# Output stores through GpSimd's queue and diagonal sums on VectorE, with a new hand-written order

## The chip, the core and the metric

The kernel runs on one core of one Trainium2 chip. The metric is the device time of one execution in microseconds (us), and for each kernel the median of its runs. The core's engines are TensorE (PE, with its weight loads as PEld), VectorE (DVE), ScalarE (ACT), GpSimd (POOL) and SyncE (SP, which here only issues DMAs). Each works through its own list of instructions in order and waits on semaphores for the others.

## What is computed

Two parts, one after the other. The first is a linear attention with a decaying state, for 4 batches, 8 heads, 768 steps and 48 dimensions. The second is a feed-forward layer of 384 to 2048 to 384 with a squared ReLU, on the attention's output of 3072 tokens.

```python
for t in range(S):                       # attention, all batches b and heads h
    cur = einsum('bhd,bhe->bhde', u[None] * kt, vt)
    y[:, :, t] = einsum('bhd,bhde->bhe', rt, state + cur)
    state = w[None, :, :, None] * state + einsum('bhd,bhe->bhde', kt, vt)
...
h = x @ w_in                             # x: 3072 x 384, from y
r = maximum(h, 0.0)
out = (r * r) @ w_out                    # 3072 x 384, float32
```

The product with u concerns a step's own k and v alone: for each token and head it is the sum over d of r·u·k, times v. This is the "diagonal" below.

## The kernel before

The 768 steps are cut into 6 chunks of 128, so that there are 24 units of one chunk and one batch: unit i has chunk i // 4 and batch i % 4. For each unit:

- r and k are loaded (`rt`, `kt`) and scaled by powers of w into one bf16 tile `rkw` (`scale`, L301 for two units at a time from unit 6 on, L303 for units 0 to 5, by VectorE).
- `rkw` is transposed into `rkT`: units 0 to 5 by TensorE (`turn`, L333, with an eviction by ScalarE, L337), later pairs by one transposing DMA (`rkD`, L322).
- `at` (L369) multiplies k and r into scores, `mask` (L377, VectorE, two per unit) keeps those before the diagonal.
- The diagonal: VectorE multiplies the two halves of `rkT` into `rk` (L357 for a pair, L360 for one unit), and four small TensorE matmuls with `uwb`, a table of u/w, add up over d: in `diag_sums` (L389) for units 0 to 3, and inside `sums` (L410), ahead of the state's product (L398), for units 4 to 23. `diag_v` (`dv`, L420) multiplies the sums with v.
- `y_mm` (`y`, L441 and L447) multiplies the scores with v and r with the state; `evict_y` (`yb`, L456) adds the diagonal's part. `yb` is transposed into `xT`: by TensorE for units 0 to 5 (`xturn`), later by a transposing DMA (`xD`, L467).
- `state_add`, `state_decay` and `state_cast` (`sadd`, `sdec`, `stb`) carry the state on.
- `mm1` (L493) is x times `w_in`, 16 blocks per unit or pair, in pieces; `relu` (L501, ScalarE), then the square by ScalarE (`sqA`, L508) or VectorE (`sqD`, L510); `mm2` (L517; L533 for the last unit, in two column ranges) is the product with `w_out`. `evict_o` (`osb`, L524) copies the result to one of six buffers named osb, and `store` (`out`, L553) writes it to the output from SP's queue.

What runs when is written out by hand. A manual schedule records the instructions in the order of the string `ORDER`; each engine gets its own part of that order. A word such as `m1.6.3@5` is the step, the unit, the piece and the PSUM bank. `fill.8` is eight matmuls of a constant tile (L216) that do nothing but keep TensorE occupied.

The loads of r and k come from SP's queue. POOL's queue carries the weights (`w_in_q`, L288, and `w_out_q`, L291, which are converted to bf16 on the way), `vt` of units 0 to 5 (L311) and two small loads (L168 and L169). A DMA that waits on SP or POOL holds up all that are behind it on the same engine.

Of the kernel before, what the change touches and what calls it, by code (L numbers as in the profile page):

```python
# [16 lines left out]
kt.0.0 kt.0.1 rt.0.0 rt.1.0 I.0 rt.1.1 vt.0 ktA.1.0 lnat.0 fill.26 log@4567 kt.1.1 lnat.1 ids rt.2.0 w.1 upper w.0  # L17
fill.8 cols@1 rt.2.1 wk scale.0.0 kt.2.0 zeros scale.0.1 wr fill.8 turn.0.0@2 kt.2.1 copied uwb turn.0.1@5 rkT.0.0
rt.3.0 rkT.0.1 vt.1 rk.0 fill.10 at.0@63 scale.1.0 rt.3.1 I.3 kb.0@4 mask.0.0 d.0@2 turn.1.0@7 I.2 kbT.0 kt.3.0
mask.0.1 rkT.1.0 vt.2 scale.1.1 vb.0 I.1 kt.3.1 fill.19 turn.1.1@4 dv.0 y.0@3 rkT.1.1 rt.4.0 yb.0 vb.1 rk.1 fill.9  # L20
kb.1@4 kt.4.0 scale.2.0 at.1@31 xturn.0@6 rt.4.1 mask.1.1 d.1@5 turn.2.0@2 xT.0 rkT.2.0 scale.2.1 kt.4.1 fill.5
m1.0.0@7 kbT.1 mask.1.0 turn.2.1@2 relu.0.0 dv.1 rt.5.0 fill.2 y.1@1 rkT.2.1 m1.0.3@4 yb.1 end rt.5.1 s.1@5
scale.3.0 relu.0.3 wend xturn.1@7 rk.2 at.2@26 xT.1 kb.2@0 mask.2.1 sqA.0.0 kt.5.0 d.2@4 turn.3.0@3 vt.3 s.0@7
sadd.1 rkT.3.0 m1.0.2@1 kt.5.1 scale.3.1 kbT.2 O.0 m1.1.0@6 mask.2.0 vb.2 relu.0.2 vt.4 turn.3.1@3 dv.2 m1.1.3@5
rt.6 rkT.3.1 sadd.0 O.1 y.2@1 relu.1.0 kt.6 m1.1.2@0 yb.2 relu.1.3 vt.5 at.3@72 rk.3 relu.1.2 kb.3@4 mask.3.1
xturn.2@6 sqA.1.0 O.2 m1.0.1@5 scale.4.0 xT.2 s.2@0 O.3 sqD.0.3 d.3@2 relu.0.1 m1.1.1@1 vb.3 mask.3.0 turn.4.0@3
kbT.3 m1.2.0@6 scale.4.1 relu.1.1 dv.3 m1.2.1@4 rkT.4.0 sqD.1.3 sqA.0.2 y.3@7 m1.2.2@1 scale.5.0 relu.2.1 sqD.1.1
m1.2.3@2 relu.2.2 sqD.0.1 s.3@5 sqA.1.2 turn.4.1@4 m2.0.0@3 sadd.3 relu.2.3 sadd.2 m2.1.0@1 rkT.4.1 yb.3 relu.2.0
m2.1.1 rk.4 vb.4 scale.5.1 kb.4@7 stb.1 xturn.3@6 at.4@42 kbT.4 m2.0.1 mask.4.1 xT.3 stb.0 s.4@5 mask.4.0 turn.5.0@6
m1.3.0@2 sqD.2.1 rkT.5.0 y.4@0 dv.4 relu.3.0 turn.5.1@6 rt.8 sadd.4 m1.3.3@7 rkT.5.1 yb.4 m2.1.2 sqA.3.0 sqA.2.0  # L30
m2.0.2 kt.8 xturn.4@2 m2.0.3 xT.4 scale.6.0 kb.5@5 osb.0 m2.1.3 scale.7.0 relu.3.3 m1.3.1@2 vtS.6 kbT.5 vb.5
m1.4.0@6 scale.6.1 scale.7.1 at.5@75 relu.4.0 m2.2.0@0 mask.5.0 osb.1 rkD.6 sqA.4.0 m1.4.1@4 sqD.2.3 sqA.2.2 sqD.3.3
m1.4.2@1 relu.3.1 mask.5.1 m2.2.1 stb.3 sdec.4 m1.4.3@6 relu.4.2 rt.10 rk.5 y.5@5 sqA.4.2 scale.8.0 s.5@2 scale.8.1
relu.4.1 m2.2.2 scale.9.0 relu.4.3 vtS.8 m1.3.2@1 sqD.3.1 stb.4 m2.3.0@4 dv.5 relu.3.2 yb.5 m2.2.3 scale.9.1 kt.10
m2.3.1 osb.2 sadd.5 sqA.4.1 m2.4.0@1 sqD.4.3 vb.6 xturn.5@0 sdec.5 at.6@2376 xT.5 rk.6 rkD.8 m2.4.1 stb.2 mask.7.0
stb.5 m1.5.0@0 sqA.3.2 mask.6.0 s.7@7 relu.5.0 mask.7.1 m1.5.3@5 mask.6.1 s.6@2 relu.5.3 m2.4.2 dv.6 out.0 vb.8
y.6@3 dv.7 rt.12 y.7@0 yb.6 m1.5.1@6 yb.7 m2.3.2 sadd.6 relu.5.1 xD.6 scale.10.0 m2.4.3 sqA.5.0 scale.10.1 sqA.5.1
m2.3.3 sadd.7 vtS.10 osb.4 m1.5.2@6 scale.11.1 scale.11.0 m2.5.0@3 relu.5.2 sqD.5.3 kt.12 m2.5.1 sqA.5.2 rk.8
at.8@1520 osb.3 sdec.6 m2.5.2 mask.9.0 rkD.10 m2.5.3 mask.8.0 s.8@4 mask.8.1 osb.5 s.9@2 m1.6.0@7 mask.9.1 m1.6.1@6
sadd.8 relu.6.0 dv.9 kt.14 m1.6.3@5 relu.6.1 dv.8 m1.6.7@1 sqA.6.0 scale.12.0 sadd.9 sqA.6.1 y.9@3 rt.14 y.8@4 vb.10  # L40
m1.6.2@0 yb.8 stb.6 m1.6.5@2 yb.9 relu.6.3 sdec.9 xD.8 m1.6.4@6 relu.6.5 scale.12.1 m2.7.0@3 relu.6.2 sqD.6.3
relu.6.7 vtS.12 m2.6.0@4 scale.13.0 relu.6.4 scale.13.1 m1.6.6@7 sqA.6.2 rk.10 at.10@6120 sqA.6.4 rkD.12 m2.6.1
relu.6.6 mask.10.0 sqA.6.5 s.10@5 sdec.7 m2.7.1 sqA.6.6 sqD.6.7 m2.7.2 stb.7 mask.10.1 stb.9 out.1 m2.7.3 sadd.10
kt.16 mask.11.0 y.10@6 osb.7 m1.8.0@1 dv.10 m1.8.1@2 rt.16 scale.14.0 relu.8.0 sdec.8 m1.8.3@5 relu.8.1 mask.11.1
m2.6.2 stb.8 yb.10 sqA.8.1 s.11@3 y.11@2 relu.8.3 dv.11 m1.8.6@1 vb.12 yb.11 m1.8.4@6 relu.8.6 sadd.11 xD.10 m2.6.3
rk.12 sqA.8.0 relu.8.4 scale.15.0 m1.8.2@2 scale.14.1 m1.8.5@0 relu.8.2 sdec.10 out.4 m2.9.0@7 osb.6 scale.15.1
vtS.14 sqA.8.2 sqD.8.3 m2.8.0@6 relu.8.5 out.3 at.12@4312 sqA.8.6 rkD.14 s.12@0 sqA.8.5 mask.13.0 m2.8.1 sqA.8.4
mask.12.1 m1.8.7@5 mask.12.0 m1.10.1@1 relu.8.7 mask.13.1 out.2 m1.10.3@3 relu.10.1 scale.16.0 vtS.16 s.13@4 sadd.12
y.12@2 dv.12 rt.18 m2.8.2 sdec.11 m1.10.6@5 yb.12 m1.10.5@0 dv.13 relu.10.6 sqD.8.7 y.13@2 stb.10 m2.9.1 relu.10.5
scale.17.0 yb.13 sqA.10.6 m2.8.3 sadd.13 relu.10.3 xD.12 m1.10.2@0 osb.8 sqD.10.3 sqA.10.1 m1.10.0@3 scale.16.1  # L50
kt.18 m1.10.7@1 relu.10.0 scale.17.1 rt.20 at.14@5642 relu.10.2 rk.14 sqA.10.0 m2.9.2 mask.15.1 vb.14 m2.9.3
mask.14.0 rkD.16 relu.10.7 m1.10.4@2 mask.14.1 sqA.10.2 mask.15.0 s.15@5 stb.11 s.14@0 sqA.10.5 m2.11.0@3 dv.14
osb.9 y.14@4 relu.10.4 y.15@6 kt.20 yb.14 vb.16 m2.11.1 sdec.12 sqA.10.4 m2.10.0@1 sadd.15 stb.12 out.5 dv.15
m1.12.0@2 sqD.10.7 m1.12.1@7 relu.12.0 yb.15 m1.12.3@4 scale.18.0 xD.14 scale.18.1 m2.10.1 relu.12.3 scale.19.0
m1.12.7@6 relu.12.1 rt.22 m2.10.2 relu.12.7 out.7 m1.12.2@7 sqA.12.0 vtS.18 sqD.12.7 m2.11.2 sdec.13 relu.12.2
scale.20.0 m1.12.6@2 sqA.12.1 kt.22 sadd.14 m1.12.4@7 scale.19.1 m1.12.5@4 scale.21.0 relu.12.4 scale.20.1 m2.11.3
relu.12.5 sqD.12.3 m2.13.0@6 sqA.12.4 rk.16 rkD.18 osb.11 at.16@4705 scale.21.1 sqA.12.2 m2.10.3 mask.16.1 relu.12.6
m1.14.7@3 sdec.15 osb.10 scale.22.0 stb.13 m2.13.1 sqA.12.5 mask.16.0 m1.14.0@7 out.10 relu.14.7 mask.17.0 out.6
# [25 lines left out]
def kernel(  # L84
# [21 lines left out]
    NH = 6  # L106
# [516 lines left out]
```

## Time and profile before

| | us |
|---|---|
| median of 3 runs | 171.85 |
| lowest and highest run | 170.75, 172.5 |
| the profiled execution | 171.94 |
| its span, from first to last instruction | 170.2 |
| PE busy in it | 163.9 |
| DVE busy in it | 122.3 |
| ACT busy in it | 129.8 |
| POOL busy in it | 15.7 |

The span and the profiled execution's time belong together: 1.74 us of that execution lie outside the span. Busy time of PE counts pipelined matmuls, so how densely it works is read from the distance between one piece and the next in the chain, not from the share.

### The profile page before, as it was taken

What the parts mean: (1) busy time and instruction counts of PE and PEld (TensorE: products, weight loads), DVE (VectorE), ACT (ScalarE), POOL (GpSimd) and SP (SyncE); (2) the same over time, 40 slices, a digit from 0 to 9 for tenths busy, and PEclk for the clock granted to TensorE, in tenths of its full rate; (3) what the DMA queues carried; (4) which work ended last, traced back from release to release, by engine and by line L of the source; (5) the groups of instructions that cost most, each with busy time, mean ns of one, the idle gap of its engine ahead of it and who ended that gap; (6) DMA issues with size and microseconds to landing.
All of it is one profiled execution on the core that took longest, in us unless ns stands there. A gap on an engine that the chain in (4) does not pass through costs nothing.

```text
span 170.2 us, 4733 instructions
## 1 busy us (share of the span) xinstructions
PE 163.9 (96%) x1947; PEld 134.1 (79%) x1947; DVE 122.3 (72%) x243; ACT 129.8 (76%) x255; POOL 15.7 (9%) x36
## 2 busy tenths in 40 slices
PE   7959999999999999999999999999999999999993
PEld 7649999778787697886977887787889789688672
DVE  6567999876999989988988888989697662101100
ACT  3735999888796489698499679688699739599921
POOL 7770670000000000000000000000000000000000
PEclk9996999999999999999999999999999999999999
DMA  3999999999999899999999997998990501100044
GB/s 92 172 279 240 272 194 254 213 201 227 185 181 218 153 214 190 181 212 191 236 182 202 174 251 173 188 288 197 180 232 4 179 6 54 42 0 4 0 164 162
DMA packets 91493, 28.86 MB, mean 170 GB/s; under 512 B 82864, under 2 KB 90672, under 8 KB 91472
## 3 DMA queue, kind: packets, MB, share of 16 engines
q1 hardware_dynamic: 88416, 23.99, 67.5%
q0 software_dynamic: 2624, 4.33, 12.9%
q8 instruction: 15, 0.25, 0.6%
q10 hardware_dynamic: 432, 0.25, 0.6%
q14 instruction: 6, 0.05, 0.1%
HBM read 20.50 MB, written 4.72 MB: 148 GB/s over the span
## 4 chain that ended last, share of the span: by engine, by line
PE 87%; DMA 6%; DVE 3%; SPq 2%; issue 1%; DVEq 0%
PE bank L493 36%; PE bank L517 34%; DMA rt<-in_r_dram 4%; PE bank L369 4%; PE bank L441 3%; DMA xT<-yb 2%; PE bank L398 2%; PE bank L447 2%; SPq L281 2%; PE bank L533 2%; PE bank L333 1%; PE bank L410 1%; PE bank L345 1%; PE bank L216 1%; PE bank L477 1%
## 5 line engine op out<-in xcount | busy, mean ns | idle before, releaser
L493 PE MATMUL bank<-xT,w_in_q 128*128 128x256 bf16 (+1 forms) x720 | 72.6, 251 | 0.1
L501 ACT ACTIVATE gr<-bank 128x512 f32<-128x512 f32 x96 | 55.3, 604 | 19.0 <-PE bank L493 15.2
L517 PE MATMUL bank<-w_out_q,g 128*128 128x384 bf16 x368 | 68.6, 326 | 0.0
L493 PEld LDWEIGHTS <-w_in_q 128*128 128x128 bf16 x720 | 63.8, 113 | 3.9 <-DMA xT<-yb 0.3
L517 PEld LDWEIGHTS <-g 128*128 128x128 bf16 x368 | 34.3, 98 | 18.1 <-issue 0.2
L508 ACT ACTIVATE g<-gr 128x512 bf16<-128x512 f32 x68 | 41.2, 636 | 0.2
L377 DVE TENSOR_TENSOR am<-bank,smask 128x512 bf16<-128x512 f32 x48 | 31.3, 684 | 7.4 <-PE bank L369 6.6
L510 DVE TENSOR_TENSOR g<-gr 128x512 bf16<-128x512 f32 x28 | 19.0, 686 | 17.2 <-ACT gr L501 17.2
L524 ACT COPY osb<-bank 128x384 f32<-128x384 f32 x23 | 11.0, 480 | 5.7 <-PE bank L517 5.6
L456 DVE TENSOR_TENSOR yb<-bank,dv 128x384 bf16<-128x384 f32 x24 | 12.9, 553 | 3.2 <-PE bank L447 2.3
L420 DVE TENSOR_TENSOR dv<-vb,bank 128x384 f32<-128x384 bf16 x24 | 13.0, 548 | 2.2 <-PE bank L410 1.4
L432 ACT CAST stb<-st 128x384 bf16<-128x384 f32 x20 | 10.2, 522 | 0.6 <-DVE st L428 0.6
L301 DVE TENSOR_TENSOR rkw<-rt,wpos 128x384 bf16<-128x384 f32 x18 | 9.8, 551 | 0.8 <-DMA rt<-in_r_dram 0.7
L301 DVE TENSOR_TENSOR rkw<-kt,wneg 128x384 bf16<-128x384 f32 x18 | 9.7, 551 | 0.8 <-DMA kt<-in_k_dram 0.8
L337 ACT COPY rkT<-bank 128x512 bf16<-128x512 bf16 x12 | 7.0, 590 | 3.4 <-PE bank L333 3.4
L216 PE MATMUL bank<-warm 128*128 128x128 bf16 x87 | 8.4, 265 | 1.1 <-DVE warm L161 1.1
L441 PE MATMUL bank<-vb,am 128*128 128x48 bf16 x192 | 8.9, 185 | 0.0
L428 DVE TENSOR_TENSOR st<-st,wend 128x384 f32<-128x384 f32 x16 | 8.8, 550 | 0.0
L424 DVE TENSOR_TENSOR st<-bank,st 128x384 f32<-128x384 f32 x16 | 8.7, 549 | 0.0
L441 PEld LDWEIGHTS <-am 128*128 128x128 bf16 x192 | 7.9, 97 | 0.8
L369 PE MATMUL bank<-rkT 64*128 64x128 bf16 x192 | 8.2, 221 | 0.2 <-ACT rkT L337 0.2
L216 PEld LDWEIGHTS <-warm 128*128 128x128 bf16 x87 | 7.0, 121 | 1.2 <-DVE warm L161 1.0
(75 smaller groups left out, 120.8 us busy)
## 6 DMA issues: line engine op xcount, KB each, us to landing
out_dram<-osb SPq DMA_DIRECT2D x23, 192.0 KB, 2.4
rt<-in_r_dram SPq DMA_DIRECT2D x9, 384.0 KB, 5.8
kt<-in_k_dram SPq DMA_DIRECT2D x9, 384.0 KB, 5.2
vt<-in_v_dram SPq DMA_DIRECT2D x9, 384.0 KB, 4.5
w_in_q<-in_moe_w_in_dram POOLq DMA_DIRECT2D x4, 384.0 KB, 8.3
w_out_q<-in_moe_w_out_dram POOLq DMA_DIRECT2D x4, 384.0 KB, 8.8
vt<-in_v_dram POOLq DMA_DIRECT2D x6, 192.0 KB, 7.3
kt<-in_k_dram SPq DMA_DIRECT2D x11, 96.0 KB, 5.2
```

What stands on the lines that cost most here:

```text
L216: nc.tensor.matmul(out=banks[0][:, :128], lhsT=warm, rhs=warm, start=True, stop=True)
L301: nc.vector.tensor_tensor(t["rkw"][:, x, :, :, :D], pair(src), pair(wneg if x else wpos), ALU.mult)
L369: nc.tensor.matmul(out=t["at"][o][:, p, :], lhsT=t["rkT"][sl, 1, p, :], rhs=t["rkT"][sl, 0, p, :], start=True, stop=True,)
L377: nc.vector.tensor_tensor(am, t["at"][o], smask.unsqueeze(1).to_broadcast([C, HP, C]), ALU.mult)
L420: nc.vector.tensor_tensor(t["dv"], t["vb"], t["d"].unsqueeze(2).to_broadcast([C, H, D]), ALU.mult)
L441: nc.tensor.matmul(out=y[:, 2 * p + o, :], lhsT=t[f"am{o}"][:, p, :], rhs=t["vb"][:, 2 * p + o, :], start=(o == 0 and p == 0), stop=c == 0 ...
L456: nc.vector.tensor_tensor(t["yb"], t["y"], t["dv"].rearrange("p h d -> p (h d)"), ALU.add)
L493: nc.tensor.matmul(out=t["h", s][:, a], lhsT=turned, rhs=chunks[c]["xT"][:, b : b + m, n, :], start=(n == 0), stop=(n == NK - 1),)
L501: nc.scalar.activation(t["gr", s], t["h", s], AF.Relu)
L508: nc.scalar.activation(g, x, AF.Square)
L510: nc.vector.tensor_tensor(g, x, x, ALU.mult)
L517: nc.tensor.matmul(out=t["o"], lhsT=chunks[units[i][0]]["g"][:, f, units[i][1], :], rhs=w_out_q[f // 4][:, f % 4, :], start=(f == 0), stop ...
```

## The change

There are three things in it.

**Stores.** `store` takes a queue. The 22 stores of units 0 to 21 become `outP`, issued by POOL; unit 22 and the two halves of unit 23 stay on SP.

**Diagonal of units 12 to 23.** Where the table has a word `dx.i`, the pair i, i+1 has no `rk` from `rkT` and no matmuls with `uwb`. VectorE multiplies r and k out of `rkw`, which has tokens on the partitions (`diag_product`, into the same buffers as `rk`), multiplies with a row of u·w that all partitions hold (`diag_weigh`), and adds up over d (`diag_add`). For this row POOL loads u and w to all 128 partitions, into two of the six osb buffers, and multiplies them (`uB`, `wB`, `uw`). `dv` is now allocated for pairs of units, two buffers deep. `sums` of units 20 to 23 has nothing left to do.

**Order.** The whole table is new. It holds 102 fills in place of 87, 72 squares on ScalarE in place of 68, and 24 on VectorE in place of 28.

The core of the diff:

```diff
+    def by_rows(i):
+        return i >= NH and f" dx.{i // 2 * 2} " in ORDER.replace("\n", " ")
+    def rows_of(i):
+        whole = two("rk", i, work, [128, HP, C], bufs=RKB)
+        return whole.rearrange("p u a c -> p u (a c)")[:, :, :dm]
+    def diag_product(i):
+        x = rkw_b[i // 2 % NPAD].rearrange("p u x a o e -> p u x (a o) e")[:, :, :, :, :D]
+        nc.vector.tensor_tensor(rows_of(i).rearrange("p u (h d) -> p u h d", h=H), x[:, :, 0], x[:, :, 1], ALU.mult)
+    def diag_weigh(i):
+        whole = of_two("dv", i, work, [C, H, D], F32, bufs=2)
+        nc.vector.tensor_tensor(
+            whole.rearrange("p u h d -> p u (h d)"), rows_of(i), uw.unsqueeze(1).to_broadcast([128, 2, dm]), ALU.mult
+        )
+    def diag_add(i):
+        whole = of_two("dd", i, work, [C, H], F32, bufs=3)
+        nc.vector.tensor_reduce(whole, two("dv", i, work, [C, H, D], F32, 2), axis=mybir.AxisListType.X, op=ALU.add)
...
+    def spread_row(name):
+        rows[name] = mpool.tile([128, dm], F32, name="osb")
+        src = dict(uB=u, wB=w)[name].rearrange("h d -> (h d)")
+        nc.gpsimd.dma_start(out=rows[name], in_=src.unsqueeze(0).to_broadcast([128, dm]))
+    def uw_row():
+        nc.gpsimd.tensor_tensor(uw, rows["uB"], rows["wB"], ALU.mult)
...
     def sums(i):
-        if not apart(i):
+        if not apart(i) and not by_rows(i):
...
     def diag_v(i):
-        t["dv"] = work.tile([C, H, D], F32, name="dv")
-        nc.vector.tensor_tensor(t["dv"], t["vb"], t["d"].unsqueeze(2).to_broadcast([C, H, D]), ALU.mult)
+        of_two("dv", i, work, [C, H, D], F32, bufs=2)
+        d = t["dd"] if by_rows(i) else t["d"]
+        nc.vector.tensor_tensor(t["dv"], t["vb"], d.unsqueeze(2).to_broadcast([C, H, D]), ALU.mult)
...
-    def store(i):
+    def store(i, queue=nc.sync):
-        nc.sync.dma_start(out=out[b * S + c * C : b * S + (c + 1) * C, :], in_=tiles[i]["osb"])
+        queue.dma_start(out=out[b * S + c * C : b * S + (c + 1) * C, :], in_=tiles[i]["osb"])
...
+        outP=lambda i: store(i, nc.gpsimd),
```

A line of the table before, and of the new one, in both of which the last products stand:

```diff
-m2.23.0@0 out.20 m2.22.3 out.19 osb.23.0 out.17 m2.23.1@1 osb.22 out.23.0 out.22 osb.23.1 out.23.1
+osb.19 outP.21 m2.22.0@7 osb.18 outP.19 m2.23.0@2 m2.23.1@4 osb.23.0 osb.20 m2.22.1 outP.20 osb.23.1 outP.18
+out.23.1 m2.22.2 outP.17 out.23.0 m2.22.3 osb.22 out.22
```

How it moves instructions is seen best at three places. Rows are one engine's instructions in their order, with line, operation, output and inputs.

The first is POOL's list at the start. Before:

```order
L169 DMA wu<-in_u_dram 4x2x48
L288 DMA w_in_q_147<-in_moe_w_in_dram 128x3x512
L311 DMA vt<-in_v_dram 128x8x48
masks.py:197 MEMSET ident_100 4x4
masks.py:199 AFFINE_SELECT ident_100<-ident_100 4x4
masks.py:197 MEMSET identb 128x128
masks.py:199 AFFINE_SELECT identb<-identb 128x128
masks.py:65 MEMSET smask 128x128
```

Now:

```order
L220 DMA wu<-in_u_dram 4x2x48
L280 DMA osb<-in_u_dram 128x384
L326 DMA vt<-in_v_dram 128x8x48 x3
masks.py:197 MEMSET ident_96 4x4
masks.py:199 AFFINE_SELECT ident_96<-ident_96 4x4
masks.py:197 MEMSET identb 128x128
masks.py:199 AFFINE_SELECT identb<-identb 128x128
L303 DMA w_in_q_142<-in_moe_w_in_dram 128x3x512
```

The first quarter of `w_in` went behind the row of u, three loads of v and the identity matrices.

The second is POOL's list some instructions later, where the weights of the second product are loaded. Before:

```order
L288 DMA w_in_q_148<-in_moe_w_in_dram 128x3x512
L268 COPY wend<-wend_c 64x4x48 x2
L311 DMA vt<-in_v_dram 128x8x48
L291 DMA w_out_q_151<-in_moe_w_out_dram 128x1536
L311 DMA vt<-in_v_dram 128x8x48
```

Now:

```order
L303 DMA w_in_q_143<-in_moe_w_in_dram 128x3x512
L326 DMA vt<-in_v_dram 128x8x48
L306 DMA w_out_q_147<-in_moe_w_out_dram 128x1536
L306 DMA w_out_q_146<-in_moe_w_out_dram 128x1536
L275 COPY wend<-wend_c 64x4x48 x2
```

The quarter of `w_out` that the second product begins with (151 before, 146 now) stood ahead of the other three and now has one of them ahead; the copies of `wend`, which wait for ScalarE, went behind both.

The third is VectorE's list where the state of a pair is carried on and the next pair is scaled, around unit 12 (`st` is a state, `am` the kept scores, `g` a square, `lnat` now holds the row of u·w, `dd` the sums over d). Before:

```order
L456 TENSOR_TENSOR yb<-bank_257,dv 128x384
L420 TENSOR_TENSOR dv<-vb,bank_79 128x384
L456 TENSOR_TENSOR yb<-bank_78,dv 128x384
L424 TENSOR_TENSOR st_3_140<-bank_79,st_3_140 128x384
L357 TENSOR_TENSOR rk<-rkT 128x1024
L301 TENSOR_TENSOR rkw_130<-rt,wpos 128x8x48
L301 TENSOR_TENSOR rkw_130<-kt,wneg 128x8x48
```

Now:

```order
L386 TENSOR_TENSOR rk<-rkw_124 128x2x384
L547 TENSOR_TENSOR g<-gr 128x2x256
L390 TENSOR_TENSOR dv<-rk,lnat 128x768
L316 TENSOR_TENSOR rkw_125<-rt,wpos 128x8x48
L316 TENSOR_TENSOR rkw_125<-kt,wneg 128x8x48
L465 TENSOR_TENSOR st_3_135<-st_3_135,wend 128x384
L316 TENSOR_TENSOR rkw_125<-kt,wneg 128x8x48
L413 TENSOR_TENSOR am_1684<-bank_255,smask 128x512
L413 TENSOR_TENSOR am_1692<-bank_77,smask 128x512
L396 TENSOR_REDUCE dd<-dv 128x16
L413 TENSOR_TENSOR am_1710<-bank_78,smask 128x512
L457 TENSOR_TENSOR dv<-vb,dd 128x384
```

One product per pair became two products and a sum, and `dv` reads `dd` in place of a PSUM bank.

More of the change, by code (lines that the diff above doesn't have):

```diff
@@ L16 @@
 ORDER = """
[L17 to L36, printed above, removed]
@@ L42 @@
[L42 to L46, printed above, removed]
@@ new lines @@
+upper rkT.0.0 turn.1.0@7 kt.2.1 scale.1.1 zeros rkT.1.0 kt.3.0 fill.6 turn.1.1@4 vt.3 rkT.0.1 scale.2.0 kt.3.1
+cols@5 rkT.1.1 copied rk.0 I.3 rt.4.0 vb.1 fill.6 at.0@53 at.1@67 uwb mask.0.1 kb.1@4 turn.2.0@2 kbT.1 rk.1 rt.4.1
+I.2 mask.1.0 end fill.7 d.1@3 rkT.2.0 d.0@1 kt.4.0 mask.0.0 I.1 dv.0 kt.4.1 vt.4 fill.12 y.0@2 mask.1.1 yb.0 O.1
+rt.5.0 scale.3.0 fill.16 xturn.0@7 O.0 y.1@5 scale.2.1 rt.5.1 s.1@4 xT.0 dv.1 vb.2 wend fill.5 turn.2.1@7 vb.3
+m1.0.0@2 kt.5.0 yb.1 rkT.2.1 O.2 relu.0.0 rk.2 kb.0@7 kt.5.1 scale.3.1 O.3 kbT.0 at.2@23 xturn.1@1 mask.2.1 rt.6
@@ L579 @@
         osb=lambda i, n=None: evict_o(i) if n is None else evict_half(i, n),
-        out=lambda i, n=None: store(i) if n is None else store_half(i, n),
+        outP=lambda i: store(i, nc.gpsimd), out=lambda i, n=None: store(i) if n is None else store_half(i, n),
     )
```

119 lines of the change are left out of this document (72 added, 47 removed).

## The prediction

> **What bounds the kernel now.** I read the page first, then busy time by stretch, then what PE waited for. The stretches' columns are stretch, length, busy PE, PEld, DVE, ACT and POOL (with counts), granted clock, DMA share and GB/s.
>
> ```profile
> PE 163.9 (96%) x1947; PEld 134.1 (79%) x1947; DVE 122.3 (72%) x243; ACT 129.8 (76%) x255; POOL 15.7 (9%) x36
> PEclk9996999999999999999999999999999999999999
> 16.30:40.00 23.70, 23.70 (x388) 20.50 (x386) 20.18 (x40) 21.93 (x48) 5.82 (x9) 1.00 1.07 227
> 40.00:80.00 40.00, 40.00 (x510) 32.18 (x509) 37.82 (x73) 32.89 (x64) 0.00 (x0) 1.00 1.00 193
> 80.00:140.00 60.00, 59.94 (x674) 48.88 (x672) 50.65 (x95) 46.12 (x88) 0.00 (x0) 1.00 0.90 180
> 140.00:167.40 27.40, 27.32 (x226) 21.53 (x223) 3.28 (x6) 21.29 (x43) 0.00 (x0) 1.00 0.17 56
> PE bank L369 <- ACT rkT L337: 0.2, 1, 0.2
>   DMA xT<-yb: 0.3, 1
> ```
>
> From 16.3 us to 167.4 PE is busy in every stretch at full clock. Its only waits there are 0.2 us for `rkT` and 0.3 us for one transposed `xT` (the last two rows: us, times, and what the weights of `w_in` waited for). So three things set the time: when the dense stretch begins, how much PE work lies in it, and what follows its end. Other engines matter where they put a hole into it. VectorE is nearest to that: idle 2.18 us in 40 to 80, and 9.35 in 80 to 140.
>
> The chain of waits shows the start (start us, length us, what):
>
> ```profile
> 3.67 6.36 DMA rt<-in_r_dram
> 10.60 0.88 DVE am L377 x2
> 13.33 0.96 PE bank L216 x9
> 16.37 0.66 PE bank L493 x11
> ```
>
> Loads of r to 10.03, VectorE's scaling and masks, then short PE work up to the first `mm1`, 16.37.
>
> **The change, part by part.** I sum against the profiled execution: 171.94 = span 170.2 + 1.74 outside. It is 0.09 from the median 171.85.
>
> *a) Diagonal matmuls gone.* Pieces of PE in the chain:
>
> ```profile
> 73.14 0.08 PE bank L410 x4
> 73.22 0.20 PE bank L398 x4
> 117.98 0.08 PE bank L410 x4
> 118.07 0.19 PE bank L398 x4
> 118.91 0.20 PE bank L441 x8
> 28.64 0.22 PE bank L333 x4
> 28.87 2.10 PE bank L517 x12
> 30.96 0.22 PE bank L345 x4
> ```
>
> Four small matmuls of L410 move PE on by 0.08 to 0.09 (117.98 to 118.07), although each reads as 0.17 long in a listing of groups: they are pipelined. Twelve units lose theirs: **-1.1 us** (12 x 0.09). This is the whole gain on PE; the 15 more fills (L216) stand ahead of the first `mm1`.
>
> *b) Start.* POOL's rows, with the time from issue to landing of each kind of load:
>
> ```profile
> 2.94 0.82 POOL L288 DMA_DIRECT2D w_in_q<-in_moe_w_in_dram  x1
> 3.72 0.96 POOL L311 DMA_DIRECT2D vt<-in_v_dram  x1
> 18.61 0.99 POOL L268 COPY wend<-wend_c 64x192 f32<-64x192 f32 x2 [6.86 <-ACT wend_c L263]
> L291 POOL DMA_DIRECT2D w_out_q<-in_moe_w_out_dram x4: 561/570/588, 20.5 to 23.9; - x4
> DMA to landing us min/median/max: 7.1/8.8/10.9
> DMA to landing us min/median/max: 7.0/8.3/11.0
> w_out_q<-in_moe_w_out_dram POOLq DMA_DIRECT2D x4, 384.0 KB, 8.8
> vt<-in_v_dram POOLq DMA_DIRECT2D x6, 192.0 KB, 7.3
> ```
>
> (The first landing row is of `w_out_q`, the second of `w_in_q`.) The first quarter of `w_in` was issued at 2.94. Now the row of u (0.6 to 0.9), three `vt` (0.9 each) and the identities (some 0.8) stand ahead: issue at about 7.2, landing 14.2 to 18.2 by the times 7.0 to 11.0. In exchange the first loads of r and k share the transfer engines with less and should land before 10.03. VectorE then has scales, two `rk` and four masks ahead of what PE needs, and PE the transposes, fills, `y.1`, `s.1` and a turn ahead of the first `mm1`. I put that `mm1` at 17.1, **+0.7**; bounds -0.8 (loads sooner by some us, half of it eaten by VectorE) to +2.2 (`w_in` at 18.2 and some waiting).
>
> Of what now stands ahead of it, `y.1` (0.20, L441), `s.1` (0.19, L398) and the turn (0.22, L333) lay in the dense stretch before, and `kb.0` (0.22, L345) goes the other way: **-0.4**.
>
> *c) First quarter of `w_out`.* It was needed at 28.87, 12.5 us after the first `mm1`, and landed at 20.46 + 7.1 = 27.6. The same twelve pieces of `mm1` still precede it, so it is needed at 17.1 + 12.5 = 29.6. Ahead of it there is now one more `vt`, the row of u (192 KB each) and another quarter (384 KB): 768 KB. From the first quarter's landing at 27.6 to the last's at 23.9 + 10.9 = 34.8 the queue carried three quarters and two `vt`, 1536 KB in 7.2 us, so 768 KB are +3.6 us. Against it, POOL's 6.86 us of waiting for `wend_c` no longer stand ahead, of which the later `w_in` eats about 4: -2.9. Landing 28.3, up to 31 if the queue gains nothing from the idle time: a wait of 0 to 2.0, and I take **+0.4**, near the low end, because the 6.86 us of idle queue are a row and the sharing is not.
>
> *d) VectorE.* The nearest rows, for bf16 and f32 operands, and ScalarE's square:
>
> ```profile
> L357 DVE TENSOR_TENSOR rk<-rkT 128x1024 bf16<-128x1024 bf16 x9 | 6.2, 684 | 0.0
> L360 DVE TENSOR_TENSOR rk<-rkT 128x512 bf16<-128x512 bf16 x6 | 2.5, 418 | 1.1 <-ACT rkT L337 1.1
> L428 DVE TENSOR_TENSOR st<-st,wend 128x384 f32<-128x384 f32 x16 | 8.8, 550 | 0.0
> L510 DVE TENSOR_TENSOR g<-gr 128x512 bf16<-128x512 f32 x28 | 19.0, 686 | 17.2 <-ACT gr L501 17.2
> L508 ACT ACTIVATE g<-gr 128x512 bf16<-128x512 f32 x68 | 41.2, 636 | 0.2
> ```
>
> The product of r and k has 768 elements in bf16: between 418 (512) and 684 (1024), 0.55 us. The weighing writes f32: 384 take 550 and 512 take 686, so 768 take 0.95. The sum over d has no row: at the rate of bf16 0.55, at twice the f32 rate's time 1.9; I take 0.95, as for any other f32 operand. A pair thus costs 2.45 and saves one 0.68 (L357). Six pairs: +10.6; four squares fewer, 4 x 0.69: -2.7; net +7.9 in 80 to 140, where 9.35 were idle. ScalarE gets 4 x 0.64 more and has 13.9 idle there. The cover holds on average; but the three steps stand in one list between scales, states and masks that PE's next piece needs, so some `yb` and `rkw` will be late by a fraction: **+0.4**, between 0 and 2.
>
> For the sum over d there is a figure elsewhere: the Trainium skill, page "VectorE: DVE Perf Modes", section "The perf-mode tier table", gives tensor_reduce only the single rate, in bf16 and f32 alike, while a tensor_tensor in bf16 may go twice as fast. The row of `rk` agrees on the second (1024 in 684 ns, where f32 takes as much for 512); no row here shows a reduce. By that rule the bf16 end is excluded and the value would be the f32 one, so that the sum would stay as it is.
>
> *e) Tail.*
>
> ```profile
> 166.43 0.91 PE bank L533 x16
> 167.36 0.29 DVE osb L545
> L524 ACT COPY osb<-bank 128x384 f32<-128x384 f32 x23 | 11.0, 480 | 5.7 <-PE bank L517 5.6
> out_dram<-osb SPq DMA_DIRECT2D x6, 192.0 KB, 1.9
> out_dram<-osb SPq DMA_DIRECT2D x1, 64.0 KB, 1.5
> ```
>
> The last piece on PE was 128 columns wide, copied by VectorE in 0.29 and stored as 64 KB, landing 1.5 after issue. Now the last piece is `m2.22.3`, copied by ScalarE in 0.48 and stored as 192 KB, 1.9 to landing: **+0.6** (0.19 + 0.4).
>
> *f) Stores from POOL.* 22 issues leave SP for an engine that was idle from 24 us on. At the 0.57 to 0.96 us that POOL's rows show for an issue they need 13 to 21 us of it, spread over some 110. What this could bring is an earlier load behind a waiting store; since PE waited once for a transfer, 0.3 us, the gain is **0** (at most -0.3).
>
> A rule speaks against this edit. The Trainium skill, page "SBUF — State Buffer", section "SBUF: two separate sides", says that a DMA from GpSimd's queue has its descriptors written by GpSimd, which is locked out while VectorE runs an operation in a two-port mode. The trace: four issues of `w_out` took 561 to 588 ns each while VectorE was nearly always busy (20.18 of 23.70 us in 16.3 to 40). By the rule taken at its worst, stores would come late and hold buffers (rival 4); by the row they cost nothing on the path.
>
> Sum: -1.1 + 0.7 - 0.4 + 0.4 + 0.4 + 0.6 + 0 = +0.6, span 170.8, time **172.5**. Term by term the likeliest case spreads over 170.9 to 173.8.
>
> **Rivals.**
>
> *1. A sooner start.* If r and k land 3 us sooner and `w_in` is not the last to come, the first `mm1` is at some 14.9, 1.5 sooner. Then -1.1 - 1.5 - 0.4 + 0.6 = -2.4: 169.5. For it: 6.36 us of the start are one wait for r, while POOL's loads fill the transfer engines. Against: `w_in` itself lands at 14.2 at the soonest. Chance 0.14.
>
> *2. VectorE becomes the bound between 80 and 140.* It decides once the three steps of a pair exceed (9.35 + 2.7) / 6 + 0.68 = 2.7 us in all; each 0.1 above is 0.6 us on the path, by way of `yb`, its transpose and the `mm1` that waits for it (the 0.3 us row is that wait). At 3.2, with the sum over d at 1.7, +3.0: 175.5, slower than before. For it: only 0.25 us of room per pair, and strided reads of `rkw`. Against: rows of the same rate. Chance 0.14.
>
> *3. Weights late.* `w_in` and `w_out` at the upper ends of b and c: +1.5 and +1.6 more than I took, part of it the same delay, so 172.5 + 2.1 = 174.6. For it: a row of u spread to 128 partitions is a new kind of load at the head of the queue, and a load of 384 KB has taken up to 11.0. Against: the first quarter took 7.1. Chance 0.15.
>
> *4. POOL's stores end last.* `outP.20`, `.18` and `.17` follow `osb.20` at up to 0.96 each, 2.9 and 1.9 to landing: 4.8, against 3 pieces of 0.65, 0.48 and 1.9 = 4.3 on the other side; if they queue behind each other, 0.9 more for each of two: +0.5 to +2.3. About 173.5 in all. Chance 0.05.
>
> That the change does not do what it says, matmuls still issued say, is excluded by the list of instructions.
>
> **Numbers.** Forecast 0.52, rivals 0.14, 0.14, 0.15 and 0.05. What a measurement can tell from no change is 1%, 1.7 us about the median: below 170.1 or above 173.6. Faster: most of rival 1 and a little of the forecast, 0.13. Slower: 0.13 each of rivals 2 and 3, 0.02 of rival 4, 0.08 from the forecast's upper end: 0.36. Same: 0.51. The range 170.0 to 175.6 leaves out half of rival 1 and the ends above 2 and 3.
>
> **What would show it.** Right: the first `mm1` at 17.1 (wrong below 16 or above 18); the first `mm2` 12.5 to 13 us after it, with a wait for a DMA of `w_out` below 1 us; the three new steps at 0.55, 0.95 and 0.95; VectorE at about 58 of 60 us in 80 to 140 with PE waiting below 1 us there; the last store of 192 KB landing some 2.4 us after PE's end. PE's pieces from first `mm1` to end take 1.5 us less than the 151 of before, apart from waits. The forecast is wrong if PE waits over 2 us in 16 to 140, or if its dense stretch begins 1.5 us sooner.

## The result, and the profile after

The changed kernel took 175.31 us (median of 4 runs, 174.66 to 176.79) against 171.51 before: ratio 1.0252, 95% interval 1.0207 to 1.0297. Repeated beside other kernels it took 174.62 against 170.76: 1.0218 (1.0176 to 1.0260). It is slower by 2 to 2.5% (the intervals reach from 1.8 to 3.0%). That is inside the range that was given, and not where the forecast, 172.5, put it. Medians here are over all executions, while the ratios leave disturbed ones out (most in e3 below, five of twelve; one of 576 us in e4), so that the two do not always agree to the last digit.

The profiled execution took 174.66 with a span of 172.6, so 2.06 us lie outside the span where 1.74 did. Its page, its busy time by stretch, and what PE waited for between 14 and 170 us:

```profile
PE 163.1 (94%) x1914; PEld 133.9 (78%) x1914; DVE 128.8 (75%) x251; ACT 132.1 (77%) x259; POOL 30.2 (18%) x61
PEclk9987999999999999999999999999999999999999
```

```profile
16.30:40.00 23.70, 23.29 (x379) 20.33 (x377) 20.43 (x41) 19.79 (x43) 4.49 (x7) 1.00 1.10 223
40.00:80.00 40.00, 39.76 (x520) 32.17 (x519) 37.91 (x73) 32.30 (x62) 2.30 (x5) 1.00 1.06 198
80.00:140.00 60.00, 60.00 (x637) 48.45 (x636) 54.84 (x99) 52.03 (x102) 5.75 (x11) 1.00 0.98 176
140.00:167.40 27.40, 27.40 (x229) 21.92 (x228) 5.36 (x10) 19.84 (x38) 3.53 (x7) 1.00 0.13 41
```

```profile
PE bank L405 <- DMA rkT<-rkw: 0.2, 1, 0.2
PE bank L405 <- ACT gr L538: 0.2, 1, 0.2
```

The columns and rows are those of the prediction. The middle is as dense as before, and VectorE, with 54.84 of 60 us busy, makes PE wait nowhere. So the loss is at the ends. Four marks show it (from the trace's start and end times; the closing is what lies between PE's end and the span's):

| profile | first mm1 | PE's end | between | closing | outside the span |
|---|---|---|---|---|---|
| before | 16.26 | 167.32 | 151.06 | 2.84 | 1.74 |
| changed | 17.92 | 167.78 | 149.86 | 4.82 | 2.06 |
| difference | +1.66 | +0.46 | -1.20 | +1.98 | +0.32 |

1.66 - 1.20 + 1.98 + 0.32 = 2.76, the 2.72 between the two executions but for rounding. The two profiles are alike in one thing that moves the first mark: in both, PE had half its clock for 3.41 us ahead of the first `mm1`, from 12.41 to 15.82 us before and from 11.93 to 15.34 in the changed kernel.

**The start.** The chain of waits of the changed kernel, two rows of its VectorE's timeline (start, length, in brackets the idle time before and what ended it), and the second one's counterpart before:

```profile
5.60 5.38 DMA rt<-in_r_dram
11.08 0.06 DVE rkw L318
11.56 0.17 DVE cols L260
11.77 0.93 PE bank L405 x16
17.00 0.48 ACT xT L518
```

```profile
11.08 0.56 DVE L318 TENSOR_TENSOR rkw<-rt,wfour 128x384 bf16<-128x384 f32 x1 [1.47 <-DMA rt<-in_r_dram]
15.99 0.56 DVE L493 TENSOR_TENSOR yb<-bank,dv 128x384 bf16<-128x384 f32 x1 [0.20 <-PE bank L478]
```

```profile
13.37 0.56 DVE L456 TENSOR_TENSOR yb<-bank,dv 128x384 bf16<-128x384 f32 x1 [0.56 <-PE bank L441]
```

The chain starts at the second half of r of unit 2, landed at 10.99. Before, it started at r of unit 1 (10.03), although r of unit 2 landed later there, at 11.92: VectorE had unit 0's masks, `dv` and `yb` ahead of it. `yb` of unit 0, which the first `mm1` needs, starts at 15.99; before, at 13.37.

**The end.** GpSimd's closing drain and SP's, as rows of the program's last line (count, ns minimum/median/maximum, first and last start). Before, then the changed kernel, then the changed kernel's last pieces in the chain, its POOL stores in the timeline and its stores in the last 10 us:

```profile
L618 POOLq DRAIN  x3: 40/98/13966, 21.5 to 169.9; - x3
L618 SPq DRAIN  x3: 7/7/13, 169.3 to 169.7; - x3
```

```profile
L656 POOLq DRAIN  x3: 46/97/4925, 166.9 to 172.3; - x3
L656 SPq DRAIN  x3: 7/7/13, 171.1 to 172.1; - x3
```

```profile
165.83 1.96 PE bank L554 x12
167.81 0.48 ACT osb L561
```

```profile
166.02 1.60 POOL L590 DMA_DIRECT2D out_dram<-osb  x3 [2.54 <-ACT osb L561]
```

```profile
out_dram<-osb POOLq DMA_DIRECT2D x5, 192.0 KB, 3.0
out_dram<-osb SPq DMA_DIRECT2D x1, 192.0 KB, 2.2
```

Behind its last DMA, GpSimd's list has a drain before GpSimd takes part in the program's end. Before, that drain began at 21.5 and lasted 13.97 us: over at 35.5, 0.7 us after the last `w_out` had landed (34.76), early in the kernel. In the changed kernel it began at 166.89 and lasted 4.93, to 171.82. (Its recorded start lies ahead of the end of the last issue, here and before, so its end is what can be read, not its length.) The last store from POOL was issued by 167.62 and landed at 170.13, 0.41 us ahead of SP's last; SP was through at 171.12, and GpSimd's next step in the program's end came 0.74 us later, at 171.86. In the kernel before, that step came 0.03 us after SP was through. The closing's +1.98 consists of +0.88 from PE's end to the last landing (2.76 against 1.88: a longer copy, 0.48 against 0.29; a larger store, which lands 2.22 us after its issue against 1.52 for 64 KB, and would take 1.86 without late stores from POOL, as e1 below shows), +0.37 in which SP still goes through its list of waits behind that landing, and +0.71 for the drain (1.96; the rest is rounding).

### The profile page after: what moved, and what is told of

Its sections match the earlier page's. It is cut to its first block, busy times and chain, and to the rows that moved or that the text cites. A ratio compares the mean times of both kernels' runs of the same rounds, so it can differ in the third digit from the quotient of the medians.

```text
span 172.6 us, 4700 instructions
## 1 busy us (share of the span) xinstructions
PE 163.1 (94%) x1914; PEld 133.9 (78%) x1914; DVE 128.8 (75%) x251; ACT 132.1 (77%) x259; POOL 30.2 (18%) x61
## 4 chain that ended last, share of the span: by engine, by line
PE 83%; DMA 9%; SPq 3%; ACT 2%; issue 1%; DVE 0%; DVEq 0%
PE bank L530 34%; PE bank L554 33%; DMA rkT<-rkw 5%; PE bank L405 4%; DMA rt<-in_r_dram 3%; SPq L296 3%; PE bank L478 2%; PE bank L484 2%; PE bank L434 2%; PE bank L214 2%; PE bank L570 2%; PE bank L348 1%; PE bank L360 1%; PE bank L514 1%; ACT vb L333 0%
## 5 line engine op out<-in xcount | busy, mean ns | idle before, releaser
L538 ACT ACTIVATE gr<-bank 128x512 f32<-128x512 f32 x96 | 56.1, 604 | 13.8 <-PE bank L530 11.9
L545 ACT ACTIVATE g<-gr 128x512 bf16<-128x512 f32 x72 | 42.9, 635 | 0.4
L590 POOL DMA_DIRECT2D out_dram<-osb x22 | 11.8, 541 | 120.0 <-ACT osb L561 119.9
L547 DVE TENSOR_TENSOR g<-gr 128x512 bf16<-128x512 f32 x24 | 16.1, 681 | 11.9 <-ACT gr L538 11.9
L214 PE MATMUL bank<-warm 128*128 128x128 bf16 x102 | 9.4, 261 | 1.1 <-DVE warm L162 1.1
L405 PEld LDWEIGHTS <-rkT 64*128 64x128 bf16 x192 | 5.8, 96 | 4.4 <-issue 3.1
L214 PEld LDWEIGHTS <-warm 128*128 128x128 bf16 x102 | 8.0, 121 | 1.2 <-DVE warm L162 1.1
```

The source lines that it names most:

```text
L214: nc.tensor.matmul(out=banks[0][:, :128], lhsT=warm, rhs=warm, start=True, stop=True)
L405: nc.tensor.matmul(out=t["at"][o][:, p, :], lhsT=t["rkT"][sl, 1, p, :], rhs=t["rkT"][sl, 0, p, :], start=True, stop=True,)
L538: nc.scalar.activation(t["gr", s], t["h", s], AF.Relu)
L545: nc.scalar.activation(g, x, AF.Square)
L547: nc.vector.tensor_tensor(g, x, x, ALU.mult)
L590: queue.dma_start(out=out[b * S + c * C : b * S + (c + 1) * C, :], in_=tiles[i]["osb"])
```

## Experiments

Ratios are to the kernel before on the same chip. Marks are from one profile each, and those of the start depend on the clock too: PE had half its clock for 3.41 us between 11.7 and 15.8 us in the profiles of e1, e2 and e4, as in the two above, for 6.83 us (10.18 to 17.01) in e5, and from 18.58 to 21.99 in e9. In the others no half clock is recorded until the last microseconds.

| run | edit | median us | ratio (95%) | first mm1 | closing |
|---|---|---|---|---|---|
| again | the changed kernel | 174.62 | 1.0218 (1.0176-1.0260) | 17.33 | 4.81 |
| e1_tail_sp | stores 17-21 on SP | 173.02 | 1.0136 (1.0080-1.0192) | 18.01 | 3.44 |
| e2_all_sp | all stores on SP | 173.15 | 1.0120 (1.0069-1.0172) | 18.28 | 3.39 |
| e3_old_pool | before + stores on POOL | 173.05 | 1.0075 (1.0033-1.0116) | 14.01 | 3.78 |
| e4_old_diag | before + diagonal by VectorE | 177.34 | 1.0355 (1.0303-1.0406) | 16.06 | 3.31 |
| e5_r2_later | e1 + scale.2.0 later | 173.12 | 1.0125 (1.0094-1.0155) | 18.76 | 3.43 |
| e8_row_alone | changed, row of u later | 172.95 | 1.0135 (1.0081-1.0190) | 16.29 | 4.83 |
| e6_row_later | e5 + row of u later | 171.41 | 1.0049 (1.0020-1.0078) | 15.94 | 3.43 |
| e7_old_end | e6 + end as before | 171.03 | 1.0036 (1.0004-1.0068) | 16.20 | 2.99 |
| e10_one_late | e7 + store 22 on POOL | 172.47 | 1.0103 (1.0057-1.0149) | 16.36 | 4.38 |
| e9_first_unit | e7 + unit 0 first, two mm1 pieces | 172.47 | 1.0101 (1.0066-1.0135) | 13.51 | 2.99 |
| e11_first_piece | e7 + unit 0 first, one piece | 171.56 | 1.0044 (1.0010-1.0079) | 14.01 | 2.99 |

### The changed kernel again

> The changed kernel itself, unaltered, so that the runs beside it stand against it on one chip. Expected 174.7 to 176.8, as its first four executions, and in its profile again GpSimd's closing drain ending 1.5 us or more after the last store from POOL has landed.

174.62, a little below the expected 174.7, and its drain ended 1.69 us after the last landing from POOL, as in the first profile. Its first `mm1`, 17.33, came at full clock.

### The tail: late stores back on SP

```diff
-outP.21 ... outP.19 ... outP.20 ... outP.18 ... outP.17
+out.21 ... out.19 ... out.20 ... out.18 ... out.17
```

> The changed kernel, with the stores of units 17 to 21 alone put back on SP at their places in the order. Theory of the tail: in the changed kernel GpSimd's closing drain ended 1.68 us after its last store had landed, and the last landing (170.54) was 2.75 us after PE's end where before it was 1.87. With no late store on POOL the drain ends long before, so the span falls from 172.6 to 171.5 to 171.9 and the median by 0.7 to 1.1 us. Rival (the tail is long because its last store is of 192 KB after a slower copy): nothing to gain, within 0.3 us of the changed kernel.

Measured: 173.02, 1.6 us below the changed kernel run again (1.4 by the ratios, whose intervals overlap a little); the closing fell by 1.38 (4.82 to 3.44). Drains of that profile:

```profile
L655 POOLq DRAIN  x3: 46/98/3941, 141.4 to 170.9; - x3
L655 SPq DRAIN  x3: 7/7/13, 170.4 to 170.7; - x3
```

GpSimd's drain was over at 145.4. Of the 1.38, 0.7 is the drain that no longer ends last, and the rest is the landing (2.4 after PE's end in place of 2.8) and fewer waits of SP behind it. The expectation named the drain alone and was too low.

```diff
-outP.0 ... outP.21
+out.0 ... out.21
```

> The changed kernel with all 22 stores of units 0 to 21 back on SP at their places in the order. Theory of the tail: as the run with five stores back, 0.7 to 1.1 us below the changed kernel, and not more, since between 16 and 168 us PE hardly waits for transfers in the changed kernel; the time outside the span shows whether the queue costs something there (2.06 us in the changed kernel, 1.74 before). Rival 1: 17 more stores on SP hold up loads behind them, so that it is slower than the run with five by 0.5 us or more. Rival 2 (stores on POOL cost throughout): faster than the run with five by 0.5 us or more.

173.15 and 1.0120 (1.0069 to 1.0172), and in the profiles a span of 171.2 us as in e1: no cost or gain of the 17 earlier stores is to be seen. The profiles speak against both rivals; the ratios alone, with intervals of half a per cent to either side, could not exclude 0.5 us. 1.88 to 1.99 us stayed outside the span, so the queue is not what made that longer.

The kernel before, with its stores of units 0 to 21 on POOL:

```diff
-        nc.sync.dma_start(out=out[b * S + c * C : b * S + (c + 1) * C, :], in_=tiles[i]["osb"])
+        (nc.gpsimd if i < 22 else nc.sync).dma_start(out=out[b * S + c * C : b * S + (c + 1) * C, :], in_=tiles[i]["osb"])
```

> The kernel before with one edit: the stores of units 0 to 21 are issued by POOL, at their places in the old order. Theory of the tail: the last of them (unit 17) is issued some 2 us before PE's end, lands near 168.5, and the closing drain ends 0.7 to 1.7 us after that, 169.3 to 170.2, where SP's part ended at 169.4: +0 to +0.8 us in the span, and 0.3 outside it if the queue costs there: 0.3 to 1.1 us slower than before. Rival (the queue is free, the new order made the tail): within 0.3 us of before.

1.0075 (1.0033 to 1.0116), about 1.3 us, a little above the range expected. Its closing grew by 0.94:

```profile
L618 POOLq DRAIN  x3: 46/98/4937, 165.7 to 171.2; - x3
L618 SPq DRAIN  x3: 7/7/13, 170.5 to 170.9; - x3
```

The drain lasted 4.94 us again, to 170.69, behind a last issue that ended at 166.57. Outside the span it lay at 1.74 to 1.86, as before.

And in the run with the old end (e7, below), one store:

```diff
-out.22
+outP.22
```

> The run with the old end, with one store alone moved from SP to POOL: that of unit 22, the last but one to be issued (165.41 us in that run's profile, with PE's end at 165.76 and SP's part over at 167.92). Theory of the tail: GpSimd's closing drain ended 4.1 to 4.2 us after the end of the last issue from POOL in the changed kernel and in the old one with stores on POOL; so here it ends at 165.4 + 0.55 + 4.2 = 170.1, and the kernel is 1.8 to 2.4 us slower, by one store. Rival (the cost comes from several stores queued behind each other on POOL): within 0.5 us of the run with the old end.

Ratio 1.0103 against 1.0036 for the run without the edit, or 1.1 us (on two chips), less than the 1.8 to 2.4 that was expected; closing 4.38 against 2.99: +1.39.

```profile
L654 POOLq DRAIN  x3: 46/98/3708, 166.0 to 170.2; - x3
```

One store is enough. Its issue ended at 166.53 and the drain at 169.68: 3.15 us later, not the expected 4.2. The 4.1 to 4.2 came where three to five stores were issued in a row; what holds across the runs with a late store is that the drain ended 1.5 to 1.7 us after the last landing from POOL (168.15 here).

### The start: an idle VectorE, or late loads

```diff
-turn.1.1@4 vt.3 rkT.0.1 scale.2.0 kt.3.1 ... mask.0.1 kb.1@4
+turn.1.1@4 vt.3 rkT.0.1 kt.3.1 ... mask.0.1 scale.2.0 kb.1@4
```

> The changed kernel with the stores of units 17 to 21 on SP (as in the run with five stores back) and one word of the order moved: the first scaling of unit 2 (scale.2.0, which needs r of unit 2) stands behind the first mask of unit 0 on VectorE, in place of ahead of the copy of the columns and of rk of unit 0. Theory of the start: in the changed kernel VectorE sat idle from 9.61 to 11.08 us for that r, with work for units 0 and 1 behind it whose inputs were there; the first mm1 came at 17.92 in place of 16.26. So the first mm1 comes 0.6 to 1.2 us sooner than with the five stores alone (18.0), and the median falls by as much. Rival (the start is late because loads or the weights w_in are): the first mm1 stays within 0.3 us.

1.0125 against 1.0136: 0.2 us by the ratios, which alone could not exclude the 0.6 that was expected. The first `mm1`, 18.76, cannot be set against e1's 18.01, since the clock was half for twice as long. What speaks against the theory besides is e6 below: it differs from e8 by this word and the late stores, and is faster by 1.5 us in the ratios, of which the stores were 1.4 in e1. With the word moved, VectorE and PE waited for something else. A row of each one's timeline in e5:

```profile
11.03 0.17 DVE L258 COPY cols<-bank 128x8 f32<-128x8 f32 x1 [1.02 <-PE bank L255]
```

```profile
9.10 0.40 PE L346 MATMUL bank<-identb,rkw 128*128 128x128 bf16 x4 [1.38 <-DVE rkw L316]
```

The columns come from PE behind the transposes of unit 1, and those wait for VectorE's scaling of r and k of unit 1, which waits for the loads.

```diff
-wu kt.0.0 kt.0.1 rt.0.0 rt.1.0 uB lnw rt.1.1
+wu kt.0.0 kt.0.1 rt.0.0 rt.1.0 lnw rt.1.1 ... uB wB
```

> The changed kernel with one edit: the load of the row of u is moved from the head of POOL's queue to beside the row of w. Theory, after the runs before: this load alone made the start late, since moving the scaling of unit 2 gave nothing and moving the row 1.7 us. So the first mm1 comes at 15.9 to 16.5 in place of 17.3 to 17.9, r of unit 2 lands before 10.0 in place of 10.9, and the median falls by 1.2 to 1.8 us from the changed kernel's 174.6, the long end staying. Rival (both edits were needed, the row only makes VectorE's wrong place visible): the first mm1 stays above 16.8 and the median above 174.

> The run before this one with one more edit: the load of the row of u to 128 partitions is moved from the head of POOL's queue to beside the row of w, after the first products. Theory of the start: VectorE's order was the cause, so this gives 0 to 0.4 us. Rival (the row of u at the head of the queue delays r and k): r and k of units 1 and 2 land 0.5 us sooner or more, and the first mm1 comes 0.5 to 1 us sooner.

(In the second of these texts, the run before this one is e5.) Alone, the row's move took the ratio from 1.0218 to 1.0135; after the moved scaling, from 1.0125 to 1.0049. Both are 1.3 to 1.4 us, so e8's theory and e6's rival hold. VectorE's row of unit 2 and the first `mm1`, in the changed kernel again and then with the row moved alone:

```profile
11.01 0.56 DVE L318 TENSOR_TENSOR rkw<-rt,wfour 128x384 bf16<-128x384 f32 x1 [0.66 <-DMA rt<-in_r_dram]
...
17.33 0.83 PE L530 MATMUL bank<-xT,w_in_q 128*128 128x128 bf16 x12
```

```profile
9.98 0.56 DVE L317 TENSOR_TENSOR rkw<-rt,wfour 128x384 bf16<-128x384 f32 x1 [0.59 <-DMA rt<-in_r_dram]
...
16.29 0.83 PE L529 MATMUL bank<-xT,w_in_q 128*128 128x128 bf16 x12
```

r of unit 2 landed at 10.92 and 9.88. VectorE's work behind it moved by 1.03 and the first `mm1` by 1.04. The landing does not hang on one profile: it was 10.92 to 11.44 in the five with the row at the head (changed, again, e1, e2, e5) and 9.69 to 9.95 in the six without (e6 to e11). So the row of u, 192 KB ahead of three `vt` on POOL's queue, made loads on SP's queue land later and the start later by a microsecond; that the two queues then compete for the same transfer engines is the likely reason, not a tested one. Why the ratios gained 0.3 to 0.4 us more than the mark moved was not settled. The clock may have a part in it: of the five profiles with the row at the head four had half clock ahead of the first `mm1`, of the six without none.

### The end of the order

```diff
-m2.23.0@2 m2.23.1@4 osb.23.0 osb.20 m2.22.1 ... m2.22.2 ... m2.22.3 osb.22 out.22
+m2.22.1 m2.22.2 m2.23.0@2 osb.20 out.20 m2.22.3 osb.23.0 out.18 out.17 m2.23.1@4 osb.22 out.23.0 out.22 osb.23.1 out.23.1
```

> The run before this one with one more edit: the last products in the sequence of the kernel before, so that the last piece on PE is the narrow half of unit 23, copied by VectorE and stored as 64 KB. Expected from the tail's rows: 0.19 us less in the copy and 0.4 less to the landing, 0.4 to 0.6 us below the run before this one. Rival (the end of SP's list of waits sets the tail, whatever is stored last): within 0.2 us. With all edits the theory expects a time 0 to 1 us below the kernel before, since 12 groups of diagonal matmuls (1.1 us) are gone and both losses with them.

In the profile the closing went from 3.43 to 2.99, the 0.4 that was expected. Between the medians it is 0.4 as well, but the ratios' intervals (1.0020 to 1.0078 and 1.0004 to 1.0068) overlap, so it is shown in the profile alone. With all edits the kernel is still not below the one before: 1.0036 (1.0004 to 1.0068).

### What is left at the start

```diff
-mask.0.1 scale.2.0 kb.1@4 turn.2.0@2 kbT.1 rk.1 ... mask.1.0 ... mask.0.0 ... dv.0 ... y.0@2 mask.1.1 yb.0
+mask.0.1 mask.0.0 kb.1@4 kbT.1 d.0@1 ... dv.0 ... y.0@2 yb.0 ... scale.2.0 rk.1 mask.1.0 ... mask.1.1
-m1.0.0@2 ... xT.1 m1.0.3@5
+m1.0.0@2 ... turn.2.1@7 m1.0.3@6
```

> The run with the old end, with VectorE's order at the start edited: both masks, dv and yb of unit 0 stand ahead of rk and the masks of unit 1, and two pieces of mm1 of unit 0 are taken forward on PE, with 35 fills there cut to 27. Theory A (VectorE's two masks and rk of unit 1 ahead of yb of unit 0 are what is left of the late start): the first mm1 comes at 14.0 to 14.8 in place of 16.2 and PE's end 0.7 to 1.5 us sooner, below the kernel before. Theory B (the start is bound by VectorE's whole work for the first units, so that the first mm1 comes sooner and PE waits later): the first mm1 is sooner, PE waits 1 us or more between 16 and 32 us, and the time stays within 0.5 us.

Theory B, and worse than the 0.5 us it allowed: 172.47. (The edit takes 40 fills down to 21, not 35 to 27: PE has 1895 matmuls here and 1914 in e7.) The first `mm1` came at 13.51, but the second piece waited for a quarter of `w_in`, and from 18.58 to 21.99 the clock was half:

```profile
13.51 0.83 PE L528 MATMUL bank<-xT,w_in_q 128*128 128x128 bf16 x12
...
17.68 0.86 PE L528 MATMUL bank<-xT,w_in_q 128*128 128x128 bf16 x12 [1.62 <-DMA w_in_q<-in_moe_w_in_dram]
```

```diff
-m1.0.0@2 ... turn.2.1@7 m1.0.3@6
+m1.0.0@2 ... xT.1 m1.0.3@5
```

> The run with unit 0's masks first, with the second piece of mm1 back at its old place, so that PE does not wait for a quarter of w_in (1.62 us at 17.68 there). Theory A (what is left of the late start is VectorE's order): PE's end 0.7 to 1.5 us sooner than in the run with the old end, median near 170. Theory B (VectorE's whole work for the first units, and the loads, bound the start): the first mm1 comes near 13.5 to 14.5 and the time stays within 0.5 us of the run with the old end (171.0).

Theory B again: first `mm1` at 14.01, PE's end at 166.31 where the run with the old end had 165.76; 152.30 us in between in place of 149.56. Behind its first `mm1` PE waited 0.6 us for VectorE's scaling, 0.7 for an `rkT` and 0.5 for a transposing DMA. A sooner first piece is no gain if what follows it is not there. No version here beats the kernel before.

### The diagonal in the old order

```diff
-rk.12 ... rk.14 ... rk.22 ... s.20 ... s.21 ... s.22 ... s.23
+uB wB uw ... dx.12 du.12 dr.12 ... dx.14 du.14 dr.14 ... dx.22 du.22 dr.22
```

> The kernel before with one edit: the diagonal of units 12 to 23 by VectorE, in the old order, its three steps where the one product of a pair stood; the row of u*w is loaded and multiplied behind the last quarter of w_out. Stores as before. If the gain on PE is 0.09 us for each of 12 groups of four matmuls and VectorE has room, -1.1 us against before. Rival (VectorE becomes the bound between 80 and 140 us, because the three steps stand in a row in a list made for one): yb late, PE waits 1 to 4 us for xT, and the time is 0 to 3 us above before.

1.0355: 6.2 us slower between the medians, more than even the rival expected. PE's waits in 80 to 140, and that stretch:

```profile
PE bank L528 <- DVE am L411: 2.2, 3, 1.3
PE bank L528 <- DVE yb L491: 1.7, 1, 1.7
PE bank L552 <- DVE g L545: 0.8, 1, 0.8
```

```profile
80.00:140.00 60.00, 55.71 (x591) 44.92 (x592) 56.42 (x102) 44.45 (x86) 0.00 (x0) 1.00 0.85 171
```

PE waited 4.7 us for VectorE. In the new order the same instructions made it wait for nothing. So edit and order cannot be priced apart here: the order is what makes room for the diagonal.

## Why the prediction was wrong, and where it was right

**Right in the main: a, c and d.** 149.86 and, again, 149.56 us between first `mm1` and PE's end are 1.2 to 1.5 less than before, as 12 x 0.09 and 0.4 of moved pieces say. No run shows the two apart, since e4, which has the first alone, had PE wait. VectorE's new steps:

```profile
L386 DVE TENSOR_TENSOR rk<-rkw 128x768 bf16<-128x768 bf16 x6 | 3.3, 546 | 0.0
L390 DVE TENSOR_TENSOR dv<-rk,lnat 128x768 f32<-128x768 bf16 x6 | 5.7, 946 | 0.0
L396 DVE TENSOR_REDUCE dd<-dv 128x16 f32<-128x768 f32 x6 | 5.7, 943 | 0.0
```

0.55, 0.95 and 0.94, as forecast. VectorE's busy time in 80 to 140 us grew by 4.2 and not by 7.9; 2.1 of the rest fell behind 140. The 0.8 us of waits in c and d were too much: PE waited 0.2 us for a transposed `rkT` and 0.2 for ScalarE, and never for `w_out`. Rival 2 did not come about. In e4 VectorE did hold PE up, but not on the condition that rival 2 names: the three steps took 0.55, 0.96 and 0.95, 2.46 together and below its 2.7, and the stretch had 3.6 us of VectorE idle. Where the steps stand in the list decided, and not how long they are.

The Trainium skill, page "VectorE: DVE Perf Modes", section "The perf-mode tier table", gives tensor_reduce the single rate alone. The trace agrees: 943 ns for 768 elements, as long as a tensor_tensor that writes f32.

**Wrong: step b**, +0.7 where +1.66 came. It said that the first loads of r and k "share the transfer engines with less" and priced the row of u as a delay of `w_in` alone. `w_in` landed at 13.8 and nobody waited for it. r of unit 1 did land sooner (7.95 against 10.03), but the new order puts r of unit 2 ahead of unit 0's product and masks, and the row of u kept that r a microsecond later than it would be without (e8). The step looked at the queue that the row stood in and not at the queue beside it. Moving the row takes back 1.04 of the 1.66; what makes the rest is open. Rival 3 named the row, with the wrong victim: no weight made PE wait. That its time, 174.6, is close to what was measured is luck.

**Wrong: steps e and f**, +0.6 and 0 where the closing grew by 1.98. The copy and the larger store are there (0.4, e7 against e6). What was missing is that a POOL store late in the kernel moves GpSimd's drain to the end of the program: 1.4 us of closing (e1, e10). Step f counted the engine's time and what stores make wait, and not what the engine still has to do behind its last DMA. Rival 4 looked at the right place, POOL's queue at the end, at a chance of 0.05 and a price of 1, but not at what happened there: its issues of up to 0.96 took 0.54, and POOL's last store landed ahead of SP's (170.13 and 170.54). What ended last was the drain behind it. Besides, the sum had nothing for the time outside the span, which grew by 0.3.

The rule that spoke against this edit did not decide. The Trainium skill, page "SBUF — State Buffer", section "SBUF: two separate sides", lets VectorE keep GpSimd from writing descriptors while it runs an operation in a two-port mode. The trace shows no sign of it: 22 issues at 541 ns on average and 559 at most, with VectorE 54.84 of 60 us busy in 80 to 140. Whether any of VectorE's operations here ran in such a mode no view shows, so the rule itself was not put to the test. What bears on the loss is the Trainium skill, page "Perfetto Trace Analysis", section "DMA Instruction — SWDGE (GPSIMD)": the end that a profile gives to such an instruction is when its descriptors are written, not when the data has moved. The trace agrees: the last issue ended at 167.62, landed at 170.13, and the drain ended at 171.82.

**Open.** With the late stores, the row, the scaling and the end of the order all edited (e7) the kernel is still 0.3 us above the one before, though PE has 1.2 to 1.5 us less to do between first `mm1` and its end. Part of it lies outside the span: 1.8 to 2.3 us in all kernels with the new diagonal, whichever queue stores, against 1.74 to 1.86 in before and e3; why was not tried. What uses up the gain on PE in the span was not found. A later start is the obvious candidate: at full clock the first `mm1` came at 14.01 in e3, whose order up to there is the old one, and at 16.20 in e7. But that mark alone does not set the end. PE's waits in e3 from 14 us on:

```profile
PE bank L369 <- DMA rkT<-rkw: 1.0, 2, 0.6
PE bank L517 <- DVE g L510: 0.7, 1, 0.7
PE bank L493 <- ACT rkT L337: 0.5, 1, 0.5
```

PE's end in e3 was 167.69, later than the 165.76 of e7. In e9 and e11 too a sooner first `mm1` brought no sooner end.

## What to carry to other kernels

Before a late DMA is moved to another engine's queue, look at what that engine must still do behind it when the program ends: here one store from GpSimd at the end made the closing 1.4 us longer, while earlier ones, whose drain was over 25 us before the end (e1), showed no cost. So stores near the end belong on the queue whose closing is shortest. A load that is needed late does not belong at the head of any queue while others wait for their first data: here it made loads on another queue land a microsecond later. And a change on a loaded engine and the order that makes room for it have to be priced together: the same three instructions per pair made PE wait for nothing in one order and for 4.7 us in the other.

## What was not expected of the hardware

- GpSimd's closing drain is recorded as 3.7 to 4.9 us long where a store had gone out late from its queue, and ended 1.5 to 1.7 us after that store had landed (the changed kernel twice, e3, e8, e10). SP's own part was through 0.2 to 0.6 us after its last landing (before, e1, and the changed kernel).
- A store of 192 KB took 1.8 to 2.0 us from issue to landing at the end of the kernel before, and 2.2 to 3.2 at the end of the changed kernel, most of them with POOL's and SP's stores under way together. Two queues are not the only reason: late in e6 stores from SP alone took up to 3.7 us.
- The granted clock of the start is not the same from one execution to the next. In the profile before, PE had half its clock from 12.4 to 15.8 us; e3, with the same order but for the queue of its stores, had the full clock throughout. Of 17 executions of the kernel before on one chip, those with a mean granted clock of 0.999 to 1.000 mostly had spans of 168.3 to 169.1 us and those with 0.987 to 0.99 of 169.4 to 170.8: about 1.3 us. The Trainium skill, page "TensorE: Matmul & The Clock Gate", section "Part 1: The HAM clock gate", ties half clock to how busy PE was in a window of some 3.4 us. The trace agrees on the length, 3.41 us; what makes one execution lose that window and another not, no run here shows.
